# Wide matmuls beside the attention in the shape of the value matmuls, and another rule for the order of TensorE's work

## The chip, the cores and the metric

The kernel runs on one core of a Trainium2 chip. The metric is device time in microseconds for one execution, the median of several runs. Five engines run side by side, each its own instructions in order: TensorE (PE; its weight loads are shown apart as PEld), ScalarE (ACT), VectorE (DVE), GpSimd (POOL) and SyncE (SP), which here issues the DMAs. They wait for each other through semaphores.

## The reference

One pre-norm transformer layer on x of 2048 rows by 1024, in bf16. What is computed:

```
h  = x + attention(layernorm(x)) @ wo        # 32 heads of 32, softmax over all 2048 keys
h2 = h + gelu_tanh(layernorm(h) @ w1 + b1) @ w2 + b2     # hidden width 3584
```

The scores are `q.k * 32**-0.5`, without a mask; the layer norms have no weights.

## The kernel before

**A planner writes the order.** The kernel is not a loop over tiles that the engines follow. Python code records tasks one by one for each engine; a `Plan` holds for each engine the time until which it is planned (`plan.free`) and for each buffer its last writer and readers, and so says from when a task could start (`plan.ready`). Each task has a cost in ns written by hand. The costs decide only the order in which instructions stand; on the chip each engine runs its list in that order and waits on semaphores.

**Stages.** First come the layer norm of x, the transposes of its rows and the first projections (to about 58 us). Then comes the attention, in four chunks of 512 queries (`CH`), each with 16 pairs of heads. All other large products are laid beside it as filling: in the first chunk the remaining projections of keys, values and queries (`fill0`, line 838); in each later chunk the output projection, the layer norm and the feed-forward part of the chunk before (`ffn`, line 1144), for the first two also the queries of a later chunk (`late_queries`). What is left and the last chunk's output projection and feed-forward part follow behind the attention as the tail.

**A unit of scores** (`qk`, line 975) is up to three matmuls of 32 contraction rows and 128 keys by 512 queries, on different rows of the array, each into a PSUM bank of its own. A pair of heads has eleven units: ten of three banks and one of two. Banks 0 to 2 and 3 to 5 take turns. One exponential on ScalarE (line 994) reads a unit's banks and writes a slot of `PT`, of which there are six. So the scores of unit u+1 can start once the exponential of unit u-1 is done with its banks.

**A value group** (`pv`, line 1008) is four matmuls of 128x32 (128 contraction rows, 32 output columns) that stand beside each other in the array, at column positions 0, 32, 64 and 96, and write four quarters of bank 6: V of two heads, and ones for the two sums of the softmax. 16 such groups make a pair of heads; then VectorE takes the bank out (`finish_pair`).

**A wide matmul** is one of 128x128 by 512. `group` (line 516) records the eight of a projection or of a hidden block of the feed-forward part, two at a time; the 28 of an output block of the feed-forward part stand in `ffn` (line 1406); one of 128 columns is in `spread` (line 642), which with `sumsq` makes the norms that the bias of the exponential needs. Beside the attention all of these share one bank, 7: the next group waits until the bank has been taken out.

**Kinds.** `pe` (line 279) records a TensorE task with a kind: "R" for scores, "C" for value groups and `sumsq`, "F" for all else. Where the kind differs from the one before, the planner adds 105 ns.

**The loop** (from line 1444) chooses the next piece of TensorE's work. It works out `q_r`, `p_r` and `f_r`: when the next scores, value group and filling could start. Filling is given out in runs of at least `FMIN` (2) pieces unless the scores are more than `LATE` (700 ns) late; scores go when their banks are free; after scores, value groups go in runs if at least `CMIN` (4) are ready, else filling; and the earliest if none is ready. If the oldest value group not done is `NPT` (6) units back, value groups go first ("block"). `qk_prereq` (line 962) makes sure, by running filling until it is there, that the norms of a new group of heads are known, and issues the DMAs of the queries (`Qd`). From the second chunk on, `quota` holds filling back once the output projection is done.

Of the kernel before, what the change touches and what calls it, by code (L numbers as in the profile page):

```python
# [8 lines left out]
ACT = mybir.ActivationFunctionType  # L9
ALU = mybir.AluOpType  # L10
AX = mybir.AxisListType
E = mybir.EngineType

P = 128
INF = float("inf")
# [186 lines left out]
def build_kernel(nc, A_x, A_wqkv, A_wo, B_w1, B_b1, B_w2, B_b2, out):  # L202
    _, S, D = A_x.shape
    F = B_w1.shape[1]
    DH = 32
    NT = S // P
# [4 lines left out]
    FC = F // P  # L211
# [5 lines left out]
    GK = GC * math.sqrt(2.0 / math.pi)  # L217
    QF = 1.2
    EARLY = 8
    RES = (1, 2, 3)  # L220
    FMIN, LATE, CMIN = 2, 700.0, 4
    CH = [(0, 512), (512, 512), (1024, 512), (1536, 512)]

    x2 = A_x[0]
# [51 lines left out]

    work = [0.0]

    def pe(fn, reads=(), writes=(), inc=True, cost=0.0, kind="F"):
        if kind == "F":  # L280
            work[0] += cost
        if mode[0] != kind:
            cost += 105.0
            mode[0] = kind
        plan.task(E.PE, fn, reads=reads, writes=writes, inc=inc, cost=cost)

    def mm(n):
        return n / 2.4 + 2.5


    base = (nc.sbuf_base + 63) // 64 * 64
# [27 lines left out]
    biasm, _ = sb("biasm", [P, G, NCH], dt.float32)  # L319
    B_bias = [[Buf() for _ in range(NCH)] for _ in range(G)]  # L320
# [63 lines left out]
    B_ps = nbufs(8)  # L384
# [131 lines left out]
    def group(mms, evac, reads_of, n=512, chunk=2, chs=()):  # L516
        bank = fbanks.next()
        k = len(mms)
        for i, (lhsT, rhs) in enumerate(mms):
            if i % chunk == 0:  # L520
                rd = []
                for j in range(i, min(k, i + chunk)):
                    rd += reads_of(j)
                yield Need(rd, [B_ps[bank]] if i == 0 else [], [c_ for c_ in chs if c_ is not None] if i == 0 else ())
            pe(lambda p, i=i, lhsT=lhsT, rhs=rhs: p.matmul(ps[:, bank, 0:n], lhsT, rhs, start=(i == 0), stop=(i == k - 1)),  # L525
               reads=reads_of(i), writes=[B_ps[bank]] if i in (0, k - 1) else [], inc=(i == k - 1), cost=mm(n))
            if i == k - 1:
                evac(bank)

# [112 lines left out]
    def spread(n_ap, B_n, out_ap, B_out, cols):  # L642
        d_ = dgi[0] % 2
        dgi[0] += 1
        bank = fbanks.next()
        dve(lambda v: v.tensor_scalar(dg[:, d_, :], ident[:], n_ap, None, ALU.mult), reads=[B_ident, B_n], writes=[B_dg[d_]], cost=230)
        yield Need([B_dg[d_]], [B_ps[bank]])
        pe(lambda p: p.matmul(ps[:, bank, 0:P], ones_pp[:], dg[:, d_, :], start=True, stop=True),
           reads=[B_ones, B_dg[d_]], writes=[B_ps[bank]], cost=mm(P))
        dve(lambda v: v.tensor_reduce(out_ap, ps[:, bank, 0:P].rearrange("p (a b) -> p a b", a=cols), AX.X, ALU.max),  # L650
            reads=[B_ps[bank]], writes=[B_out], cost=290)

# [322 lines left out]
    def qk(u):  # L975
        ci, p_, un = units[u]
        w = CH[ci][1]
        g, tc = p_ // 2, CH[ci][0] // 512
        s0 = 3 * (u % 2)
        s = qdl[(ci, p_)]  # L980
        banks = sorted({b for _, _, b, _ in un})
        wr = [B_ps[s0 + b] for b in banks]
        n = len(un)
        for i, (kt, h, b, o) in enumerate(un):
            rg = h + 2 * (kt % 2)
            pe(lambda p, kt=kt, rg=rg, b=b, o=o: p.matmul(  # L986
                ps[:, s0 + b, o:o + w], K2[32 * rg:32 * rg + 32, p_, kt // 2, :], Qd[32 * rg:32 * rg + 32, s, 0:w],
                start=True, stop=True, tile_position=(32 * rg, 0), skip_group_check=True),
                reads=[B_Qd[s][0], B_Qd[s][1], B_K2h[p_][kt // 4][kt % 2]],
                writes=wr if i in (0, n - 1) else [], inc=(i == n - 1), cost=mm(w) if i % 3 == 0 else 4, kind="R")  # L990
        o_ = u % NPT
        nb = len(banks)
        wa = 512 if n != 2 or w == 512 else w
        act(lambda a: a.activation(PT[:, o_, 0:nb, 0:wa], ps[:, s0:s0 + nb, 0:wa], ACT.Exp, bias=biasm[:, g, tc:tc + 1], scale=SCALE),  # L994
            reads=wr + [B_bias[g][tc]], writes=[B_PT[o_]], cost=180 + 0.833 * nb * wa)
        for kt, h, b, o in un:
            kts.setdefault((ci, p_, kt), {})[h] = (u, b, o)
            if len(kts[(ci, p_, kt)]) == 2:
                d_ = kts.pop((ci, p_, kt))
                pending.append((ci, p_, kt, d_[0], d_[1]))  # L1000
# [143 lines left out]
    def ffn(ci, tail):  # L1144
# [163 lines left out]
        def hidden(fc, c0, c1):  # L1308
# [7 lines left out]
            def evac(bank):  # L1316
# [12 lines left out]
                else:  # L1329
                    st.append((E.DVE, lambda v: v.tensor_tensor(tm[gs][:, 0:n], xh[:, gs, 0:n], xh[:, gs, 0:n], ALU.mult), [Bx], [Bt], 80 + .65 * n))  # L1330
                st.append((E.DVE, lambda v: v.scalar_tensor_tensor(tm[gs][:, 0:n], tm[gs][:, 0:n], GB, xh[:, gs, 0:n], ALU.add, ALU.mult),  # L1331
                           [Bt, Bx], [Bt], 80 + 1.2 * n))
                st.append((E.Activation, lambda a: a.activation(tm[gs][:, 0:n], tm[gs][:, 0:n], ACT.Tanh, scale=GK), [Bt], [Bt], 180 + .75 * n))  # L1333
                st.append((E.DVE, lambda v: v.scalar_tensor_tensor(gT[:, fc, c0:c1], tm[gs][:, 0:n], 1.0, xh[:, gs, 0:n], ALU.add, ALU.mult),  # L1334
                           [Bt, Bx], B_out, 80 + 1.2 * n))
                g_ch[(fc, c0)] = chain(st)
# [57 lines left out]
        for hf in range(2):  # L1394
            turns = []
            for d4 in range(4):
                db = hf * 4 + d4
                s = w2s[db]
                bank = fbanks.next()
                for fc in range(FC):  # L1400
                    if fc == 6:
                        load_w2(db + len(B_w2_) - 1)
                    if fc % 2 == 0:
                        yield Need(B_gT[fc] + B_gT[fc + 1] + [B_w2_[s]], [B_ps[bank]] if fc == 0 else [],
                                   [g_ch[k_] for u_ in (fc, fc + 1) for k_ in ((u_, 0), (u_, 256)) if k_ in g_ch])
                    pe(lambda p, fc=fc, s=s, bank=bank: p.matmul(ps[:, bank, 0:w], w2[:, s, fc, :], gT[:, fc, 0:w],  # L1406
                                                                 start=(fc == 0), stop=(fc == FC - 1)),
                       reads=B_gT[fc] + [B_w2_[s]], writes=[B_ps[bank]] if fc in (0, FC - 1) else [], inc=(fc == FC - 1), cost=mm(w))
                dve(lambda v, bank=bank, db=db: v.tensor_scalar(oT[:, db, 0:w], ps[:, bank, 0:w], b2f[:, db:db + 1], None, ALU.add),  # L1409
                    reads=[B_ps[bank], Bf_b2f], writes=[B_oT[db]], cost=690)  # L1410

                def turn(db=db, hf=hf, d4=d4):
                    dma_t(ost[:, hf * 4:hf * 4 + 4, d4 * P:(d4 + 1) * P], oT[:, db, :], 131072, [B_oT[db]], [B_od[db]])
                turns.append(chain([("call", turn, [B_oT[db]], [B_od[db]], 0)]))
# [21 lines left out]

    fbanks.items = [7]
    fbanks.i = 0
    state["gens"].append(fill0())
    state["left"] = (8 * len(v_left) + 7 * 32 + 3 * 64 + 12 * 8) * mm(512)  # L1440
    u = 0
    ph = 0
    seg, nf = None, 0
    while u < NU or pending:
        t = plan.free[E.PE]
        service(t)
# [27 lines left out]
                break  # L1474
        quota = state["left0"] * QF * (u - state["u0"] + 1) / state["nu"] + 2000.0
        f_r = fill_ready() if (ph == 0 or ("wo", ph - 1) not in marks or state["left0"] - state["left"] < quota) else INF
        def pvs(n):
            for _ in range(max(1, n)):
                pv()

        if block:
            pvs(npv)
            seg = "C"
            continue
        late = t - q_r
        if seg == "F" and nf < FMIN and f_r <= t + 60 and late < LATE:
            nf += 1
            do_fill()
            continue
        if q_r <= t + 60:  # L1490
            qk(u)
            u += 1
            seg, nf = None, 0
            continue
        if seg is None:
            ends = npv and pending[npv - 1][2] == NT - 1
            if npv >= CMIN or ends or (npv >= 2 and f_r > t + 100):
                pvs(npv)
                seg = "C"
                continue  # L1500
            if f_r <= t + 100:
                do_fill()
                seg, nf = "F", 1
                continue
        elif seg == "F":
            if f_r <= t + 60:
                do_fill()
                nf += 1
                continue
        elif f_r <= t + 60 and q_r > t + 350:  # L1510
            do_fill()
            seg, nf = "F", 1
            continue
        best = min(q_r, p_r if p_r + 330 < q_r or q_r == INF else INF, f_r)
        if best == INF:
            if pending:
                pv()
                seg = "C"
            elif not do_fill():
                raise RuntimeError("stuck")  # L1520
        elif best == q_r:
            qk(u)
            u += 1
            seg, nf = None, 0
        elif best == f_r:
            do_fill()
            seg, nf = "F", 1
        else:
            pvs(npv)
            seg = "C"  # L1530

    rings = [([7, 6], 0), ([0, 1, 2, 3, 4, 5], 0)]
    both = [state, dict(state, gens=deque([ffn(len(CH) - 1, True)]), need=None, gen=None)]
# [113 lines left out]
```

## Time and profile before

| | |
|---|---|
| median of 3 runs | 1227.95 us (1225.98 to 1229.10) |
| the profiled execution | 1226.59 us, its span 1224.8 us |
| mean granted TensorE clock | 0.993 |
| TensorE, ScalarE, VectorE, GpSimd busy | 1185.8, 1116.5, 646.5, 26.8 us |
| exponentials (line 994) | 704, 995.9 us busy, first start 58.2, last end 1105.8 us |
| value matmuls (line 1023) | 2048 with V and 2048 with ones |
| score matmuls (line 986) | 2048 |
| TensorE instructions | 9297 matmuls, 9297 weight loads |

Busy time is the union of the instructions' times. On TensorE and ScalarE an instruction begins before the one ahead of it has ended, so the length of one is more than its price in a row of equal ones: that is read from the distance of their starts. "Idle before" is the time in which the engine stood still ahead of an instruction, and the name behind the arrow is the instruction that ended it.

### The profile page before, as it was taken

The numbers are of one execution on the slowest core, as the hardware profiler recorded it, in microseconds if no ns is written. First come the engines' busy times: TensorE is split into PE (matmuls) and PEld (weight loads), VectorE is DVE, ScalarE is ACT, GpSimd is POOL, SyncE is SP. The second block draws the span as 40 slices with busy tenths as digits, with TensorE's granted clock in tenths as the row PEclk, the third lists the DMA queues.
The fourth block names the chain that finished last, engine by engine and source line by source line (L and its number), as shares of the span: only waits on it lengthen the run. The fifth ranks groups of instructions, "written<-read, shape, count | busy, mean of one in ns | idle before, by whom it ended". The sixth has DMA issues, their size and how long they took to land.

```text
span 1224.8 us, 22862 instructions
## 1 busy us (share of the span) xinstructions
PE 1185.8 (97%) x9297; PEld 406.3 (33%) x9297; DVE 646.5 (53%) x1228; ACT 1116.5 (91%) x927; POOL 26.8 (2%) x132
## 2 busy tenths in 40 slices
PE   4999999999999999999999999999999999999999
PEld 2433323233233333333233333333223333325544
DVE  7734444444565888222366885223567852327851
ACT  5799999999999999999999999999999999994830
POOL 1100000000010000000010000000100000000000
PEclk9999999999999999999999999999989999998999
DMA  7253322223341234343622351542322613424921
GB/s 227 49 135 71 73 53 57 57 54 102 70 87 57 79 93 101 78 117 78 170 60 78 90 138 33 108 112 59 89 78 73 158 42 74 101 60 147 288 73 52
DMA packets 294840, 113.96 MB, mean 93 GB/s; under 512 B 206928, under 2 KB 292048, under 8 KB 294736
## 3 DMA queue, kind: packets, MB, share of 16 engines
q1 hardware_dynamic: 294736, 112.51, 35.8%
q8 instruction: 73, 1.20, 0.4%
q14 instruction: 31, 0.25, 0.1%
HBM read 85.21 MB, written 4.19 MB: 73 GB/s over the span
## 4 chain that ended last, share of the span: by engine, by line
PE 81%; DVE 8%; ACT 5%; issue 3%; SPq 1%; DMA 1%; POOL 0%; DVEq 0%; ACTq 0%
PE ps L525 30%; PE ps L1023 17%; PE ps L986 15%; PE ps L1406 13%; ACT PT L994 5%; PE ps L1378 4%; SPq L256 1%; DVE lnst L462 1%; DVE xh L1324 1%; DVE QT L1053 1%; DVE Rg L1043 1%; PE ps L1216 1%; DVE tm L1331 0%; DVE Rg L1049 0%; PE ps L505 0%
## 5 line engine op out<-in xcount | busy, mean ns | idle before, releaser
L994 ACT ACTIVATE PT<-ps,biasm 128x1536 bf16<-128x1536 f32 (+1 forms) x704 | 995.9, 1538 | 13.4 <-PE ps L986 12.1
L1023 PE MATMUL ps<-PT,V 128*32 128x512 bf16 x2048 | 285.5, 385 | 0.3 <-ACT PT L994 0.2
L1023 PE MATMUL ps<-PT,ones 128*32 128x512 bf16 x2048 | 285.8, 386 | 0.0
L986 PE MATMUL ps<-Qd,K 32*128 32x512 bf16 x2048 | 275.3, 386 | 7.7 <-ACT PT L994 6.1
L525 PE MATMUL ps<-hnT,w 128*128 128x512 bf16 x672 | 173.1, 382 | 3.4 <-DVE xh L1324 2.9
L1406 PE MATMUL ps<-gT,w 128*128 128x512 bf16 x672 | 173.2, 382 | 0.3 <-DVE xh L1324 0.3
L986 PEld LDWEIGHTS ps<-Qd,K 32*128 32x128 bf16 x2048 | 68.1, 91 | 297.0 <-issue 156.4
L1023 PEld LDWEIGHTS ps<-PT,V 128*32 128x32 bf16 x2048 | 77.7, 95 | 138.4 <-issue 87.5
L1036 DVE COPY Sg<-ps 128x512 f32<-128x512 f32 x64 | 44.3, 692 | 146.9 <-PE ps L1023 146.9
L525 PE MATMUL ps<-xnTe,wk 128*128 128x512 bf16 x384 | 98.6, 387 | 3.2 <-ACT xnTe L567 1.3
L1324 DVE TENSOR_SCALAR xh<-ps,b1f 128x512 bf16<-128x512 f32 x84 | 63.0, 750 | 50.1 <-PE ps L525 49.6
L525 PEld LDWEIGHTS ps<-hnT,w 128*128 128x128 bf16 x672 | 52.9, 97 | 91.0 <-issue 35.6
L1406 PEld LDWEIGHTS ps<-gT,w 128*128 128x128 bf16 x672 | 52.4, 97 | 81.3 <-issue 34.7
L1023 PEld LDWEIGHTS ps<-PT,ones 128*32 128x32 bf16 x2048 | 78.0, 95 | 0.4
L1409 DVE TENSOR_SCALAR oT<-ps,b2f 128x512 bf16<-128x512 f32 x24 | 18.0, 751 | 113.3 <-PE ps L1406 113.2
L525 PE MATMUL ps<-xnTl,wk 128*128 128x512 bf16 x256 | 65.3, 381 | 0.4
L1331 DVE SCALAR_TENSOR_TENSOR tm<-tm,xh 128x512 bf16<-128x512 bf16 x84 | 58.0, 691 | 2.4
L1334 DVE SCALAR_TENSOR_TENSOR gT<-tm,xh 128x512 bf16<-128x512 bf16 x84 | 57.1, 684 | 2.7 <-ACT tm L1333 2.4
L1333 ACT ACTIVATE tm<-tm 128x512 bf16<-128x512 bf16 x84 | 54.3, 650 | 3.8 <-DVE tm L1331 3.5
L525 PE MATMUL ps<-hnT,w_t 128*128 128x512 bf16 (+1 forms) x288 | 48.8, 332 | 0.0
L525 PEld LDWEIGHTS ps<-xnTe,wk 128*128 128x128 bf16 x384 | 31.9, 99 | 50.8 <-issue 20.8
L1378 PE MATMUL ps<-w_t,gT 128*128 128x512 bf16 (+1 forms) x252 | 48.6, 355 | 0.0
(121 smaller groups left out, 798.1 us busy)
## 6 DMA issues: line engine op xcount, KB each, us to landing
w<-in_B_w_dram SPq DMA_DIRECT2D x42, 512.0 KB, 3.8
w<-in_B_w_dram SPq DMA_DIRECT2D x24, 896.0 KB, 5.7
wk<-in_A_wqkv_dram SPq DMA_DIRECT2D x32, 256.0 KB, 3.8
Qd<-QT SPq DMA_DIRECT2D x128, 64.0 KB, 2.6
w_t<-in_B_w_dram SPq DMA_DIRECT2D x14, 512.0 KB, 6.5
w_t<-in_B_w_dram SPq DMA_DIRECT2D x8, 896.0 KB, 7.2
xr<-in_A_x_dram SPq DMA_DIRECT2D x16, 256.0 KB, 5.2
K<-kst SPq DMA_DIRECT2D x128, 32.0 KB, 1.9
```

Of the source, the lines that this page charges most:

```text
L525: pe(lambda p, i=i, lhsT=lhsT, rhs=rhs: p.matmul(ps[:, bank, 0:n], lhsT, rhs, start=(i == 0), stop=(i == k - 1)), reads=reads_of(i), write ...
L986: pe(lambda p, kt=kt, rg=rg, b=b, o=o: p.matmul(ps[:, s0 + b, o:o + w], K2[32 * rg:32 * rg + 32, p_, kt // 2, :], Qd[32 * rg:32 * rg + 32, ...
L994: act(lambda a: a.activation(PT[:, o_, 0:nb, 0:wa], ps[:, s0:s0 + nb, 0:wa], ACT.Exp, bias=biasm[:, g, tc:tc + 1], scale=SCALE), reads=wr ...
L1023: pe(lambda p, c0=c0, lhsT=lhsT, uu=uu, b=b, o=o: p.matmul(ps[c0:c0 + 32, OD, 0:w], lhsT, PT[:, uu % NPT, b, o:o + w], start=start, stop=stop,
L1036: dve(lambda v: v.tensor_copy(Sg[:, pr, 0:w], ps[:, OD, 0:w]), reads=[B_ps[OD]], writes=[B_Sg[pr]], cost=690)
L1324: dve(lambda v: v.tensor_scalar(xh[:, gs, 0:n], ps[:, bank, 0:n], b1f[:, fc:fc + 1], 0.5, ALU.add, ALU.mult), reads=[B_ps[bank], Bf_b1f], ...
L1331: st.append((E.DVE, lambda v: v.scalar_tensor_tensor(tm[gs][:, 0:n], tm[gs][:, 0:n], GB, xh[:, gs, 0:n], ALU.add, ALU.mult), [Bt, Bx], [Bt ...
L1333: st.append((E.Activation, lambda a: a.activation(tm[gs][:, 0:n], tm[gs][:, 0:n], ACT.Tanh, scale=GK), [Bt], [Bt], 180 + .75 * n))
L1334: st.append((E.DVE, lambda v: v.scalar_tensor_tensor(gT[:, fc, c0:c1], tm[gs][:, 0:n], 1.0, xh[:, gs, 0:n], ALU.add, ALU.mult), [Bt, Bx], ...
L1378: pe(lambda p, fc=fc, bank=bank, c0=c0, c1=c1, hf=hf, rows=rows: p.matmul(ps[:, bank, 0:c1 - c0], gT[:, fc, rows], w2h[hf][0][:, fc, c0:c1 ...
L1406: pe(lambda p, fc=fc, s=s, bank=bank: p.matmul(ps[:, bank, 0:w], w2[:, s, fc, :], gT[:, fc, 0:w], start=(fc == 0), stop=(fc == FC - 1)), r ...
L1409: dve(lambda v, bank=bank, db=db: v.tensor_scalar(oT[:, db, 0:w], ps[:, bank, 0:w], b2f[:, db:db + 1], None, ALU.add), reads=[B_ps[bank], ...
```

## The change

The change has three parts.

1. Beside the attention (`narrow[0]` is true from before the loop until after it) every wide matmul that opens a bank there is recorded by a new function `wide` as four of 128x32, at the four column positions, with the same moving operand and a quarter of the weights each. They write the four quarters of the bank and have the kind "C", that of the value groups. A bank that was opened in one form is finished in it.
2. The loop loses its runs. Scores go as soon as their banks are free by the plan; then value groups if the oldest not done is five units back (`LAG`) or the next one ends a pair of heads; then filling; and the earliest if none is ready. Value groups go one at a time.
3. Costs of the planner: 97 in place of 105 ns for a change of kind, 145 + 0.8333 per element in place of 180 + 0.833 for an exponential, 95 + 0.83 in place of 180 + 0.75 for a tanh. The three further matmuls of a wide one cost the planner nothing.

```diff
@@ -218,7 +218,7 @@
     RES = (1, 2, 3)
-    FMIN, LATE, CMIN = 2, 700.0, 4
+    LAG = 5
@@ -276,16 +276,31 @@
-    def pe(fn, reads=(), writes=(), inc=True, cost=0.0, kind="F"):
-        if kind == "F":
+    def pe(fn, reads=(), writes=(), inc=True, cost=0.0, kind="F", fill=False):
+        if kind == "F" or fill:
             work[0] += cost
         if mode[0] != kind:
-            cost += 105.0
+            cost += 97.0
             mode[0] = kind
...
+    narrow = [False]
+    opened = {}
+
+    def wide(bank, c0, n, lhsT, rhs, start, stop, reads, writes, inc):
+
+        if start:
+            opened[bank] = narrow[0]
+        if not opened[bank]:
+            pe(lambda p: p.matmul(ps[:, bank, c0:c0 + n], lhsT, rhs, start=start, stop=stop), reads=reads, writes=writes, inc=inc, cost=mm(n))
+            return
+        for c in range(4):
+            pe(lambda p, c=c: p.matmul(ps[32 * c:32 * c + 32, bank, c0:c0 + n], lhsT[:, 32 * c:32 * c + 32], rhs, start=start, stop=stop,
+                                       tile_position=(0, 32 * c), skip_group_check=True),
+               reads=reads, writes=writes if c in (0, 3) else [], inc=inc and c == 3, cost=mm(n) if c == 0 else 0, kind="C", fill=True)
@@ -522,8 +537,7 @@
-            pe(lambda p, i=i, lhsT=lhsT, rhs=rhs: p.matmul(ps[:, bank, 0:n], lhsT, rhs, start=(i == 0), stop=(i == k - 1)),
-               reads=reads_of(i), writes=[B_ps[bank]] if i in (0, k - 1) else [], inc=(i == k - 1), cost=mm(n))
+            wide(bank, 0, n, lhsT, rhs, i == 0, i == k - 1, reads_of(i), [B_ps[bank]] if i in (0, k - 1) else [], i == k - 1)
@@ -645,8 +659,7 @@
-        pe(lambda p: p.matmul(ps[:, bank, 0:P], ones_pp[:], dg[:, d_, :], start=True, stop=True),
-           reads=[B_ones, B_dg[d_]], writes=[B_ps[bank]], cost=mm(P))
+        wide(bank, 0, P, ones_pp[:], dg[:, d_, :], True, True, [B_ones, B_dg[d_]], [B_ps[bank]], True)
@@ -992,7 +1005,7 @@
-            reads=wr + [B_bias[g][tc]], writes=[B_PT[o_]], cost=180 + 0.833 * nb * wa)
+            reads=wr + [B_bias[g][tc]], writes=[B_PT[o_]], cost=145 + 0.8333 * nb * wa)
@@ -1330,7 +1343,7 @@
-                st.append((E.Activation, lambda a: a.activation(tm[gs][:, 0:n], tm[gs][:, 0:n], ACT.Tanh, scale=GK), [Bt], [Bt], 180 + .75 * n))
+                st.append((E.Activation, lambda a: a.activation(tm[gs][:, 0:n], tm[gs][:, 0:n], ACT.Tanh, scale=GK), [Bt], [Bt], 95 + .83 * n))
@@ -1403,9 +1416,8 @@
-                    pe(lambda p, fc=fc, s=s, bank=bank: p.matmul(ps[:, bank, 0:w], w2[:, s, fc, :], gT[:, fc, 0:w],
-                                                                 start=(fc == 0), stop=(fc == FC - 1)),
-                       reads=B_gT[fc] + [B_w2_[s]], writes=[B_ps[bank]] if fc in (0, FC - 1) else [], inc=(fc == FC - 1), cost=mm(w))
+                    wide(bank, 0, w, w2[:, s, fc, :], gT[:, fc, 0:w], fc == 0, fc == FC - 1,
+                         B_gT[fc] + [B_w2_[s]], [B_ps[bank]] if fc in (0, FC - 1) else [], fc == FC - 1)
@@ -1436,11 +1448,11 @@
+    narrow[0] = True
...
@@ -1474,60 +1486,35 @@
...
         if block:
-            pvs(npv)
-            seg = "C"
+            pv()
             continue
-        late = t - q_r
-        if seg == "F" and nf < FMIN and f_r <= t + 60 and late < LATE:
-            nf += 1
-            do_fill()
-            continue
         if q_r <= t + 60:
             qk(u)
             u += 1
-            seg, nf = None, 0
             continue
-        if seg is None:
-            ends = npv and pending[npv - 1][2] == NT - 1
-            if npv >= CMIN or ends or (npv >= 2 and f_r > t + 100):
-                pvs(npv)
-                seg = "C"
-                continue
...
+        oldest = min(pending[0][3][0], pending[0][4][0]) if pending else u
+        first_c = npv and (u - oldest >= LAG or pending[npv - 1][2] == NT - 1)
+        if first_c and p_r <= t + 60:
+            pv()
+            continue
+        if f_r <= t + 60:
             do_fill()
-            seg, nf = "F", 1
             continue
-        best = min(q_r, p_r if p_r + 330 < q_r or q_r == INF else INF, f_r)
+        best = min(q_r, p_r, f_r)
...
-        else:
-            pvs(npv)
-            seg = "C"
+    narrow[0] = False
```

More of the change, by code (lines that the diff above doesn't have):

```diff
@@ L1476, in build_kernel @@
         f_r = fill_ready() if (ph == 0 or ("wo", ph - 1) not in marks or state["left0"] - state["left"] < quota) else INF
-        def pvs(n):
-            for _ in range(max(1, n)):
-                pv()
         if block:
-            pvs(npv)
-            seg = "C"
-            continue
-        late = t - q_r
-        if seg == "F" and nf < FMIN and f_r <= t + 60 and late < LATE:
-            nf += 1
-            do_fill()
+            pv()
             continue
@@ L1492, in build_kernel @@
             u += 1
-            seg, nf = None, 0
             continue
-        if seg is None:
-            ends = npv and pending[npv - 1][2] == NT - 1
-            if npv >= CMIN or ends or (npv >= 2 and f_r > t + 100):
-                pvs(npv)
-                seg = "C"
-                continue
-            if f_r <= t + 100:
-                do_fill()
-                seg, nf = "F", 1
[L1504 to L1510, printed above, removed]
+        oldest = min(pending[0][3][0], pending[0][4][0]) if pending else u
[4 more added lines that the diff above has]
+        if f_r <= t + 60:
             do_fill()
-            seg, nf = "F", 1
             continue
-        best = min(q_r, p_r if p_r + 330 < q_r or q_r == INF else INF, f_r)
+        best = min(q_r, p_r, f_r)
         if best == INF:
@@ L1523, in build_kernel @@
             u += 1
-            seg, nf = None, 0
-        elif best == f_r:
+        elif best == p_r:
+            pv()
+        else:
             do_fill()
-            seg, nf = "F", 1
-        else:
-            pvs(npv)
-            seg = "C"
+    narrow[0] = False
     rings = [([7, 6], 0), ([0, 1, 2, 3, 4, 5], 0)]
```

## The prediction

> **What bounds the kernel now.** I read the page first (engine shares, clock slices, the chain), then ScalarE's timeline and waits, then TensorE's timeline, then a table of short windows around the two dips of the clock.
>
> ```profile
> span 1224.8 us, 22862 instructions
> ...
> PE 1185.8 (97%) x9297; PEld 406.3 (33%) x9297; DVE 646.5 (53%) x1228; ACT 1116.5 (91%) x927; POOL 26.8 (2%) x132
> ...
> PEclk9999999999999999999999999999989999998999
> ...
> q8 instruction: 73, 1.20, 0.4%
> ...
> PE 81%; DVE 8%; ACT 5%; issue 3%; SPq 1%; DMA 1%; POOL 0%; DVEq 0%; ACTq 0%
> ...
> L994 ACT ACTIVATE PT<-ps,biasm 128x1536 bf16<-128x1536 f32 (+1 forms) x704 | 995.9, 1538 | 13.4 <-PE ps L986 12.1
> ```
>
> The chain puts 81% on TensorE, but ScalarE is just as full beside the attention. Its timeline (start, length, count):
>
> ```profile
> 432.20 2.95 ACT L994 ACTIVATE PT<-ps,biasm 128x1536 bf16<-128x1536 f32 x2
> 435.05 0.63 ACT L1333 ACTIVATE tm<-tm 128x512 bf16<-128x512 bf16 x1
> 435.57 2.97 ACT L994 ACTIVATE PT<-ps,biasm 128x1536 bf16<-128x1536 f32 x2
> 438.41 0.64 ACT L1333 ACTIVATE tm<-tm 128x512 bf16<-128x512 bf16 x1
> ...
> 499.08 61.51 ACT L994 ACTIVATE PT<-ps,biasm 128x1536 bf16<-128x1536 f32 x44 [0.19 <-PE ps L986]
> ```
>
> Two exponentials go from 435.57 to 438.41, so one starts 1.423 us after the other; the lengths overlap. A tanh takes 0.52 (435.05 to 435.57), an exponential over two banks 0.996. The page's 704 are 640 of three banks and 64 of two, and 84 tanh lie among them: 640 x 1.423 + 64 x 0.996 + 84 x 0.520 = 1018.1 us. The first exponential starts at 58.2, the last ends at 1105.8: 1047.6. So 29.3 us are lost there. Taking each start against the shortest distance, 18.8 of them stand before exponentials released by scores (the waits show 12.1 of that as idle), 6.1 before tanh released by VectorE, 4.3 are a few ns per instruction.
>
> TensorE's timeline:
>
> ```profile
> 400.25 0.39 PE L986 MATMUL ps<-Qd,K 32*128 32x512 bf16 x3
> 400.57 0.60 PE L525 MATMUL ps<-hnT,w 128*128 128x512 bf16 x2
> 401.11 0.39 PE L1023 MATMUL ps<-PT,V 128*32 128x512 bf16 x2
> 401.12 0.39 PE L1023 MATMUL ps<-PT,ones 128*32 128x512 bf16 x2
> 401.34 0.38 PE L1023 MATMUL ps<-PT,V 128*32 128x512 bf16 x2
> 401.34 0.38 PE L1023 MATMUL ps<-PT,ones 128*32 128x512 bf16 x2
> 401.55 0.38 PE L1023 MATMUL ps<-PT,V 128*32 128x512 bf16 x2
> 401.56 0.38 PE L1023 MATMUL ps<-PT,ones 128*32 128x512 bf16 x2
> 401.87 0.39 PE L986 MATMUL ps<-Qd,K 32*128 32x512 bf16 x3
> ```
>
> Groups of one kind follow each other after 0.216 us, the first pair of a run after 0.226; this holds for one 128x128 matmul and for four 128x32 alike. Wherever the kind changes the distance is 0.31 to 0.32 (scores 400.25, wide 400.57), so a change costs 0.09 to 0.11, 0.105 where scores are on one side. In the built order of before I count, between the first score and the last value matmul, 1580 changes. With those distances TensorE has 1007 us of work there, 1016 with the 10 ns: as much as ScalarE's 1018. Neither has slack, and each stall of one costs the other.
>
> Windows (TensorE, its loads, VectorE, ScalarE, GpSimd, granted clock, DMA):
>
> ```profile
> 884.00:888.00 4.00, 2.75 (x35) 0.70 (x31) 1.03 (x3) 4.00 (x4) 2.00 (x11) 1.00 0.00 0
> 888.10:894.90 6.80, 6.19 (x36) 1.22 (x33) 1.78 (x4) 6.80 (x5) 0.24 (x2) 0.50 0.42 96
> 1099.70:1109.90 10.20, 9.52 (x53) 2.18 (x46) 3.17 (x6) 6.14 (x5) 0.00 (x0) 0.50 0.24 78
> ```
>
> Where wide work had run out (TensorE busy 2.75 of 4.00 us) the clock was halved soon after.
>
> **Kind changes.** The built order of the changed kernel has 1399 changes in place of 1580, all between scores and the rest: 181 x 0.105 = 19 us less on TensorE. Wide matmuls in that stretch fall from 2172 to 2144. Pricing the new order with the same distances gives 983 us, 990 with the 10 ns per run, against ScalarE's unchanged 1018. By query chunk (new TensorE / ScalarE): 238/243, 249/258, 251/258, 246/258. Pair of heads by pair, the sum of the larger of the two is 1027 before and 1020 now.
>
> **Four for one.** 2144 wide matmuls become 8576 narrow ones, with as many weight loads. At 0.216 a group this costs nothing; the row for it is the value matmuls, same shape, same array tiles, no slower in their fifth group than in their second. Bounds: -0.003 (by the rows' spread) and +0.010 us a group, the distance between the first and the third start of a group (401.11, 401.12), were it not hidden: 21 us. I take 0, the back-to-back row being the nearest. The Trainium skill (TensorE: Matmul & The Clock Gate, Measured speedup vs the span model) gives four packed matmuls a span of one plus some 4 ns for each further one, 12 ns; on every group that would be an estimated 26 us. This trace shows the offset inside a group, but not in the distance of groups.
>
> **Scores as soon as a bank is free.** This moves no work; it moves when ScalarE is served. Losses of over 0.4 us before an exponential are ten, together 10.7 us: one is the clock (0.64 at 895), the others lie where the order has two score units back to back, both banks drained, or where a norm or a DMA forces them. The order of before has ten such double units after the first, the new one three (units 132, 176, 554). Unit 176 cost 1.9 before, the mean is 1.07; I take 1.7 each, 5.1, and 0.6 for the clock, which units 576 to 584, with one or two value groups each and no wide work, should halve again. The other 8.1 us are small; they go with the saturated pairs, whose excess over ScalarE falls from 9 to 2, so I keep 2.7. Of 18.8, 8.4 stay: 10.4 saved. Bounds: 18.8 if all goes, 0 if the stalls only move. Scores now wait at the head of TensorE's queue, with values and wide work behind them; a late tanh (6.1, kept) stops TensorE too, which its 27 us of slack cover. Values may lag five units of six PT slots; one slot is left, about 1.4 us, against 0.43 for two groups, so I cost it at nothing.
>
> **The tail.** One whole output block of the third chunk's feed-forward, 28 wide matmuls, is left and goes after the attention as 128x128: 28 x 0.216 = 6.0 us. TensorE has no gap there before (busy to 1221.9), so all of it counts. After the last scores stand 15 groups (2 value, 8 wide, 5 value), 3.4 us, against 2.4 of exponentials: TensorE ends 1.0 after ScalarE, 0.6 before (1106.44): +0.4. Wide work now runs to the end, so the dip at 1099.7 should not come; of it 4.1 us at half speed lay behind the last exponential, with 0.2 on the last value group: -2.2. Sum +4.2.
>
> **Other edits.** The planner's new costs for exponential and tanh change only the order, counted above. DMAs, their queues and VectorE's instructions keep their number; SP's queue is moved past nothing. Instructions fetched rise from 1.20 MB by 15783/9297 to 2.0 MB: a packet every 8 us in place of 16; nothing in the trace waits for one.
>
> **Sum.** 1226.6 (the profiled execution, span 1224.8 and 1.8 around it) - 10.4 + 4.2 = 1220.4. It lies 1.4 below the median of the three runs, 1227.95 (1225.98 to 1229.10). I predict 1221. Under 0.3%, 3.7 us, I call it no change.
>
> **Rivals.**
>
> The stalls only move (chance 0.17). Norms and late Qd transfers force scores in both orders, as at unit 176. For it: the largest three losses (2.3, 2.2, 1.9) are of that sort. Against: three drained places for ten. Then 1226.6 + 4.2 = 1231 at worst, 1227 with half the gain.
>
> The offset adds (0.09). If the 10 ns inside a group came on top of each narrow group, TensorE has 990 + 21 = 1011 us, the balance of before, and the gain goes: about 1230. Against: the back-to-back rows. The Trainium skill's rule above (same page and section) leads here too; by its 12 ns the estimate is 1235.
>
> TensorE can't be fed (0.16, slower). A narrow group takes eight instructions in 0.216 us; before, a unit of scores, values and wide work had about 24 in 1.42 us, now 43. If issue or fetch is slower in the long run than in the short bursts of value matmuls, the groups stretch. With 0.030 us more, 64 us, TensorE has 1054 and bounds: with the 18 us of other losses kept, 1072 in place of 1047.6, so 1226.6 + 24 + 4 = 1255. It decides from about 0.013 a group, where TensorE's work is level with ScalarE's 1018 again and only the tail's +4.2 is left. Against: no growth within a run of five; nothing in the trace tells of longer ones, which now go to nine.
>
> Half clock for longer (0.06). If units 576 to 584 bring two or three dips of 6.8 to 10.2 us, with wide work queued behind, each costs up to 5 us: 1224 to 1230.
>
> **Chances.** My own case has 0.52, by itself 1214 to 1225. 0.46 of it and small parts of the first and last rivals (0.06) give faster 0.52; its other 0.06, most of those two rivals (0.15) and two thirds of the offset (0.06) give no change 0.27; the feeding rival, the last third of the offset and the worst of the moved stalls give slower 0.21. Range 1212 to 1235: under it lies the case that all 18.8 go, above it most of the feeding rival.
>
> **What would show it.** In the changed profile: narrow wide groups 0.216 us apart, in long runs too; exponentials 1.423 apart with the idle time before them down from 13.4 to about 6; first to last exponential about 1037; a half clock near units 576 to 584 and none at the end; 28 of the block's matmuls after the last exponential. Groups over 0.23 apart, or ScalarE waiting for value matmuls, would make me wrong.

## The result: slower by 0.7%

The median went from 1228.53 to 1236.69 us (1236.32 to 1237.70), a ratio of 1.0071 with a 95% interval of [1.0053, 1.0088]. The forecast was 1221, in a range of 1212 to 1235: wrong in sign. The page of the changed kernel, in the lines that answer to those shown before:

```profile
span 1234.6 us, 35830 instructions
...
PE 1189.8 (96%) x15783; PEld 428.2 (35%) x15783; DVE 647.9 (52%) x1228; ACT 1117.2 (90%) x927; POOL 26.6 (2%) x132
...
PEclk9999999999999999999999999999989999999999
...
q8 instruction: 124, 2.03, 0.7%
...
PE 81%; DVE 12%; ACT 3%; issue 2%; DMA 1%; POOL 0%; SPq 0%; DVEq 0%; ACTq 0%
...
L1007 ACT ACTIVATE PT<-ps,biasm 128x1536 bf16<-128x1536 f32 (+1 forms) x704 | 996.3, 1545 | 15.0 <-PE ps L999 10.7
```

The chain now has 12% on VectorE in place of 8%, and the idle time before exponentials is 15.0 us in place of 13.4. From the first to the last exponential it takes 1050.9 us (58.3 to 1109.2) in place of 1047.6; from there to the end 125.4 in place of 119.0. So of 9.8 us between the two profiled executions (1236.4 and 1226.6), 3.3 lie beside the attention and 6.4 behind it.

The narrow groups are not what costs. A run of eight wide matmuls in TensorE's timeline, between value groups:

```profile
1107.37 0.38 PE L1036 MATMUL ps<-PT,V 128*32 128x512 bf16 x2
1107.38 0.38 PE L1036 MATMUL ps<-PT,ones 128*32 128x512 bf16 x2
1107.59 1.90 PE L301 MATMUL ps<-gT,w 128*32 128x512 bf16 x32
1109.31 0.38 PE L1036 MATMUL ps<-PT,V 128*32 128x512 bf16 x2
```

From 1107.59 to 1109.31 there are eight groups, 0.215 us each: no offset and no growth. What TensorE now does more often stands in a stretch of the first feed-forward block (start, length, engine, line; idle time before in brackets):

```profile
440.37 0.60 PE L301 MATMUL ps<-hnT,w 128*32 128x512 bf16 x6
...
441.03 0.75 DVE L1337 TENSOR_SCALAR xh<-ps,b1f 128x512 bf16<-128x512 f32 x1 [1.11 <-PE ps L301]
...
441.44 0.39 PE L1036 MATMUL ps<-PT,V 128*32 128x512 bf16 x2
...
441.83 0.12 PEld L301 LDWEIGHTS ps<-hnT,w 128*32 128x32 bf16 x8 [0.29 <-DVE xh L1337]
441.84 0.40 PE L301 MATMUL ps<-hnT,w 128*32 128x512 bf16 x4
```

The last wide group in bank 7 starts at about 440.59, VectorE begins to take the bank out 0.43 later and is done at 441.78, and the next filling starts at 441.84, right behind it. Behind the value group of 441.44 it could have started at 441.66: 0.18 us of TensorE's time lost. Call it an evacuation when VectorE takes bank 7 out. Over the attention I took each start of a group on TensorE against the shortest distance for its kinds and summed what an evacuation of bank 7 released: 7.4 us before, 24.0 after. (The sum depends on where the line is drawn: all first groups that start within 0.16 us of an evacuation's end give 10 and 33.) Of the next fillings 18 of 207 started within 75 ns of the evacuation's end before, 83 of 205 after. And the waits reach ScalarE: before, ten exponentials lost over 0.4 us, 10.7 us together, and ahead of the scores of one of them TensorE had waited for bank 7; in the changed kernel seventeen did, 14.4 us together, and ten of them had such a wait ahead.

For a hidden block of the feed-forward part the planner reckons from the last matmul's start to the next filling 216 (matmul) + 90 (hop) + 714 (evacuation) + 90 (hop) = 1110 ns. The trace has 433 from the last matmul's start to the evacuation where VectorE was idle (417 with whole wide matmuls), some 742 for the evacuation (751 for a hidden block, 691 for most others, which the planner reckons with 690) and at least 53 to the next matmul: 1228. The bank is ready some 0.12 us later than planned, and all of that lies ahead of the evacuation, 433 against 306: from its start on, 751 + 53 = 804 ns are just what was planned. The new loop gives out filling as soon as the plan says it is ready (up to 60 ns ahead of that, `f_r <= t + 60`); the old one had mostly put something else there.

### The profile page after: what moved, and what is told of

It reads as the page before. It is cut to its first block, busy times and chain, and to the rows that moved or that the text cites. A ratio compares the mean times of both kernels' runs of the same rounds, so it can differ in the third digit from the quotient of the medians.

```text
span 1234.6 us, 35830 instructions
## 1 busy us (share of the span) xinstructions
PE 1189.8 (96%) x15783; PEld 428.2 (35%) x15783; DVE 647.9 (52%) x1228; ACT 1117.2 (90%) x927; POOL 26.6 (2%) x132
## 3 DMA queue, kind: packets, MB, share of 16 engines
q8 instruction: 124, 2.03, 0.7%
## 4 chain that ended last, share of the span: by engine, by line
PE 81%; DVE 12%; ACT 3%; issue 2%; DMA 1%; POOL 0%; SPq 0%; DVEq 0%; ACTq 0%
PE ps L301 36%; PE ps L1036 19%; PE ps L999 15%; PE ps L298 6%; PE ps L1391 4%; ACT PT L1007 2%; DVE Rg L1056 2%; DVE xh L1337 1%; DVE Sg L1049 1%; DVE lnst L477 1%; DVE QT L1066 1%; DVE tm L1344 1%; DVE Rg L1062 1%; DVE rcp L1059 1%; DVE gT L1347 0%
## 5 line engine op out<-in xcount | busy, mean ns | idle before, releaser
L1007 ACT ACTIVATE PT<-ps,biasm 128x1536 bf16<-128x1536 f32 (+1 forms) x704 | 996.3, 1545 | 15.0 <-PE ps L999 10.7
L1036 PE MATMUL ps<-PT,V 128*32 128x512 bf16 x2048 | 330.0, 386 | 0.8 <-DVE Sg L1049 0.4
L1036 PE MATMUL ps<-PT,ones 128*32 128x512 bf16 x2048 | 330.2, 386 | 0.0
L301 PE MATMUL ps<-hnT,w 128*32 128x512 bf16 x2688 | 176.8, 382 | 5.0 <-DVE xh L1337 3.0
L301 PE MATMUL ps<-gT,w 128*32 128x512 bf16 x2576 | 173.2, 380 | 0.9 <-DVE oT L1421 0.6
L1036 PEld LDWEIGHTS ps<-PT,V 128*32 128x32 bf16 x2048 | 80.6, 95 | 142.5 <-issue 113.0
L301 PEld LDWEIGHTS ps<-hnT,w 128*32 128x32 bf16 x2688 | 63.1, 96 | 81.9 <-issue 25.0
L301 PEld LDWEIGHTS ps<-gT,w 128*32 128x32 bf16 x2576 | 62.8, 96 | 66.6 <-issue 9.5
L301 PE MATMUL ps<-xnTe,wk 128*32 128x512 bf16 x1184 | 79.3, 381 | 1.5 <-DVE kst L637 0.5
L301 PE MATMUL ps<-xnTl,wk 128*32 128x512 bf16 x864 | 58.5, 381 | 0.5 <-DVE kmax L663 0.2
L600 DVE CAST kst<-ps 128x512 bf16<-128x512 f32 x28 | 19.3, 691 | 57.6 <-PE ps L301 57.5
```

Of the source, the lines that this page charges most:

```text
L301: pe(lambda p, c=c: p.matmul(ps[32 * c:32 * c + 32, bank, c0:c0 + n], lhsT[:, 32 * c:32 * c + 32], rhs, start=start, stop=stop, tile_posit ...
L1036: pe(lambda p, c0=c0, lhsT=lhsT, uu=uu, b=b, o=o: p.matmul(ps[c0:c0 + 32, OD, 0:w], lhsT, PT[:, uu % NPT, b, o:o + w], start=start, stop=stop,
```

## Experiments

The theory (bank): the narrow groups are free, and the saving is lost in these waits. Rivals: the narrow shape hurts in itself (shape), or the new planner costs spoil the order (costs). In the table "attention" is from the first to the last exponential's end, "behind" from there to the span's end, "bank" the waits for evacuations of bank 7, worked out as above; all three are of the profiled execution. Ratios are to the kernel before as it ran beside each kernel; its medians there were 1226.2 to 1228.5. In the traces of "before, held 120 ns", "changed, held, wide whole" and "before, new costs" some 150 wide matmuls are not recorded: the 6.1 of the first is rough, and "bank" stays open for the other two, as for the last two kernels.

| kernel | median us | ratio to before | attention | bank | behind |
|---|---|---|---|---|---|
| before | 1228.5 | | 1047.6 | 7.4 | 119.0 |
| changed | 1236.7 | 1.0071 [1.0053, 1.0088] | 1050.9 | 24.0 | 125.4 |
| old order, narrow | 1222.5 | 0.9954 [0.9935, 0.9972] | 1044.6 | 11.4 | 118.7 |
| changed, held 120 ns | 1221.9 | 0.9961 [0.9946, 0.9976] | 1038.3 | 8.1 | 123.6 |
| changed, held 300 ns | 1222.2 | 0.9962 [0.9949, 0.9975] | 1038.6 | 7.5 | 122.7 |
| changed, old costs | 1244.0 | 1.0138 [1.0123, 1.0153] | 1065.5 | 31.4 | 118.2 |
| before, held 120 ns | 1225.7 | 0.9981 [0.9970, 0.9992] | 1046.7 | 6.1 | 119.2 |
| changed, held, wide whole | 1250.3 | 1.0182 [1.0166, 1.0198] | 1066.6 | | 123.9 |
| old loop, narrow, new costs, held | 1221.2 | 0.9950 [0.9934, 0.9966] | 1042.8 | 9.2 | 118.2 |
| before, new costs | 1231.3 | 1.0034 [1.0025, 1.0043] | 1041.6 | | 129.2 |
| old loop as above, queries earlier | 1220.6 | 0.9951 [0.9935, 0.9968] | 1042.8 | | 119.2 |
| changed, held, queries earlier | 1223.3 | 0.9974 [0.9965, 0.9983] | 1040.1 | | 123.4 |

**The narrow shape alone, in the old order.** `wide` of the change put into the kernel before; for the planner all four keep the old kind, the first with the cost of a whole one, so that nothing moves.

```diff
+        for c in range(4):
+            pe(lambda p, c=c: p.matmul(ps[32 * c:32 * c + 32, bank, c0:c0 + n], lhsT[:, 32 * c:32 * c + 32], rhs, ...),
+               ..., cost=mm(n) if c == 0 else 0, kind="F")
```

> The order of before, instruction for instruction, with each wide matmul beside the attention as four of 128x32 in its place (the planner still counts it as a wide one, so no task moves). On the array the changes between wide and value work vanish: 1385 in place of 1580, 195 x about 0.1 = 19 us less for TensorE (991 against 1008 from the built orders). Bank theory (the narrow groups are free; the changed kernel lost its saving in waiting for the evacuation of bank 7, because the new loop gives out filling the moment the planner says and the planner says so about 0.12 us too early): the old order keeps other work between two fillings, so most of the saving comes through, 1217 to 1224 against 1228.5 before. Shape theory (narrow wide groups themselves hurt: they end later, load worse or crowd the others): no faster than before, 1228 to 1236. Cost theory (the planner's new costs spoilt the order): says the same as the bank theory here.

1222.5, faster by 0.46%: the shape theory falls. Yet 195 changes fewer, 19 us of TensorE's work, brought 3.0 us beside the attention in the profiled execution (1223.7, near the slow end of four) and some 5 to 6 in the medians. ScalarE still loses 26.3 us there (29.3 before), 17.7 of them before exponentials that scores ended: in the same order, the norms and DMAs that force scores stay where they were, and the waits for bank 7 rose by 4.0.

**Filling held in the planner.** In the changed kernel, a piece of filling that opens a bank counts as ready 120 or 300 ns later.

```diff
-        return plan.ready(E.PE, nd.reads, nd.writes)
+        return plan.ready(E.PE, nd.reads, nd.writes) + (120.0 if nd.writes and narrow[0] else 0.0)
```

> The changed kernel, but the planner holds a piece of filling that opens a bank for 120 ns longer; that is the distance by which the trace's chain (last matmul of a group to the first of the next in bank 7: 433 + 742 + 53 = 1228 ns) exceeds the planner's 1110. Bank theory: TensorE's waits for evacuations in the attention fall from 24 us to 8 to 14, next fillings within 0.15 us of an evacuation's end from 151 of 205 to under 90, time 1226 to 1233 (1236.7 unheld). Shape and cost theories: no change, 1235 to 1238, as 22 wide matmuls are still left for the tail in place of 28.

> As with 120, but held for 300 ns. Bank theory: waits for evacuations under 6 us, time 1223 to 1231, no worse than with 120. Shape and cost theories: 1235 to 1238, or slower, since filling is given out later for nothing (16 wide matmuls left for the tail).

1221.9 and 1222.2. Both beat the expectation of the bank theory, and the two rivals fall. The waits drop from 24.0 to 8.1 and 7.5; fillings within 75 ns of the evacuation from 83 to 25 and 16. (Two numbers missed: with 120 ns I had expected under 90 fillings within 0.15 us, and 99 came; with 300 ns under 6 us of waits.) The attention takes 1038.3, 12.6 less than unheld. Unheld, about 4 us of that were lost before exponentials to scores, 3.3 to a late norm and 4.6 before tanh. Held, nine exponentials lost over 0.4 us, and ahead of none of them had TensorE waited for bank 7. The hold also moves other pieces of the order (22 wide matmuls are left for the tail, not 28), so that the whole 12.6 us come from these waits isn't shown; that the hold pays and that the waits fall with it is. The same place in the block with 120 ns:

```profile
436.18 0.61 PE L301 MATMUL ps<-hnT,w 128*32 128x512 bf16 x8
...
436.84 0.75 DVE L1337 TENSOR_SCALAR xh<-ps,b1f 128x512 bf16<-128x512 f32 x1 [0.69 <-PE ps L301]
...
437.61 0.39 PE L1036 MATMUL ps<-PT,V 128*32 128x512 bf16 x2
...
437.71 0.23 PEld L301 LDWEIGHTS ps<-hnT,w 128*32 128x32 bf16 x8
...
437.83 0.39 PE L301 MATMUL ps<-hnT,w 128*32 128x512 bf16 x4
```

Value groups fill the evacuation until 437.59, and the next filling starts 0.22 behind the last of them, without a wait. The exponentials' row, held:

```profile
L1007 ACT ACTIVATE PT<-ps,biasm 128x1536 bf16<-128x1536 f32 (+1 forms) x704 | 997.8, 1593 | 10.6 <-PE ps L999 9.4
```

**The planner's old costs in the changed kernel.**

```diff
-            cost += 97.0
+            cost += 105.0
...
-            ..., cost=145 + 0.8333 * nb * wa)
+            ..., cost=180 + 0.833 * nb * wa)
...
-                ..., 95 + .83 * n))
+                ..., 180 + .75 * n))
```

> The changed kernel with the three planner costs of before (105, 180 + 0.833, 180 + 0.75). By the built order nothing of the feed-forward block is left for the tail (641 matmuls there, as before, in place of 669). Bank theory: waits for evacuations stay above 18 us and the first to last exponential at 1048 us or more; only the tail's 6 us are won, less what the attention now takes for 28 more wide matmuls: 1230 to 1238. Cost theory: the loss goes, 1222 to 1229.

1244.0, slower than both theories allowed. The costs theory falls outright: the new costs were worth 7 us. The bank theory had its 31.4 us of waits, but not how far the attention would grow, to 1065.5: that is 14.6 us more for 7.4 us more of waits. ScalarE's losses beside the attention, tanh included, rise from 32.6 to 47.1, those before exponentials that scores ended from 16.3 to 27.4. The exponentials' row has more waits for scores in it:

```profile
L1007 ACT ACTIVATE PT<-ps,biasm 128x1536 bf16<-128x1536 f32 (+1 forms) x704 | 1001.9, 1518 | 17.8 <-PE ps L999 15.9
```

What fits, though only argued: an exponential that the planner takes for 1.46 us (180 + 0.833 x 1536) while the chip takes 1.423 lets it lay more work between two scores than there is room for.

**The hold on the kernel before.** The same line in the old loop, nothing else.

> The kernel before (wide matmuls whole, old loop, old costs) with filling that opens bank 7 held 120 ns longer by the planner, and nothing else. Bank theory: the old loop waits little for evacuations (7 us in the attention, 36 of 207 next fillings within 0.15 us of an evacuation's end), so there is little to win: 1223 to 1230 against 1227.4. If the hold is simply good for any order, whatever the loop, it gains here as much as on the changed kernel (about 1%): 1213 to 1218.

1225.7, faster by 0.19%, in the expected range. The hold repairs the new loop (1.2%); in the old one it is worth little.

**Whole wide matmuls in the new order.** The changed kernel, held, with one matmul in place of the four; the order is the same.

```diff
-        for c in range(4):
-            pe(lambda p, c=c: p.matmul(ps[32 * c:32 * c + 32, ...], lhsT[:, 32 * c:32 * c + 32], rhs, ...), ..., kind="C", fill=True)
+        pe(lambda p: p.matmul(ps[:, bank, c0:c0 + n], lhsT, rhs, start=start, stop=stop),
+           reads=reads, writes=writes, inc=inc, cost=mm(n), kind="C", fill=True)
```

> The changed kernel with the 120 ns hold, but each wide matmul whole (128x128) on the array again, in exactly the same order (the planner still counts it as of the value groups' kind). By the built order 1857 changes of kind in place of 1395: 462 x 0.1 = 44 us more for TensorE (1032 against 989), above ScalarE's 1018. If four for one is free and saves the changes: TensorE bounds, first to last exponential 1060 to 1085 in place of 1038, time 1243 to 1268. If narrow groups carried a cost of their own of 0.01 us or more (21 us): half of that or less, 1222 to 1240.

1250.3, attention 1066.6: 28 us more for 44 us of changes, as expected if four for one is free. In this order the narrow shape is worth 2.3%.

```profile
L1005 ACT ACTIVATE PT<-ps,biasm 128x1536 bf16<-128x1536 f32 (+1 forms) x704 | 1000.0, 1521 | 27.2 <-PE ps L997 23.6
```

**The old loop with everything else.** The first experiment's kernel, with the four told to the planner as kind "C", the new costs and the 120 ns hold.

> The loop of before with four narrow matmuls for a wide one, told to the planner as of the value groups' kind, with the new costs and the 120 ns hold. By the built order 1391 changes and nothing of the feed-forward block left for the tail. If the rule of the new loop (scores at once, values singly) brings nothing beyond fewer changes, this should reach 1038 to 1042 from first to last exponential with a tail of 118 to 119: 1215 to 1220. If the new loop's rule is what keeps scores on time, it stays near the old order with narrow matmuls: 1220 to 1225.

1221.2: in the second expectation, near its lower end. The attention takes 1042.8, 4.5 more than in the new loop held, but nothing is left for the tail, 118.2 behind it in place of 123.6. The two come out within each other's interval: what the new loop wins beside the attention it hands back as wide matmuls that are left over. That it serves ScalarE better by its rule doesn't follow. One wait for queries, before the exponential at 607.7, costs the old loop 5.3 us, more than the whole difference, and the new loop held has none there:

```profile
607.26 0.75 PE L999 MATMUL ps<-Qd,K 32*128 32x512 bf16 x6 [2.35 <-DMA Qd<-QT]
```

**The new costs in the kernel before.**

```diff
-            cost += 105.0
+            cost += 97.0
...
-            ..., cost=180 + 0.833 * nb * wa)
+            ..., cost=145 + 0.8333 * nb * wa)
```

(and the tanh's, as in the change)

> The kernel before with the planner's three costs of the change (97, 145 + 0.8333, 95 + 0.83) and nothing else; 1557 changes in place of 1580. The changed kernel lost 7 us when it got the old costs, because a planner that takes an exponential for 1.46 us where the chip takes 1.423 lays too much of TensorE's work between two scores. If that holds for the old loop too, losses before exponentials fall: 1219 to 1225 against 1227.4. If the old loop is guarded by its own runs, no change: 1225 to 1230.

1231.3, a miss. The attention did shrink, by 6.0 to 1041.6, but 10 us more lie behind it. TensorE's timeline from the last scores on shows where, and two lines of SP's say why:

```profile
1098.74 0.39 PE L986 MATMUL ps<-Qd,K 32*128 32x512 bf16 x2
1099.06 5.35 PE L1406 MATMUL ps<-gT,w 128*128 128x512 bf16 x24
...
1111.26 0.39 PE L1224 MATMUL ps<-wo(1, 0)_99,QT 128*128 128x512 bf16 x1 [1.23 <-DVE QT L1053]
...
1127.31 7.08 PE L525 MATMUL ps<-hnT,w_t 128*128 128x256 bf16 x48 [3.85 <-DMA w_t<-in_B_w_dram]
```

```profile
1108.99 14.31 SPq L256 DMA_DIRECT2D out_dram<-ost  x4
1123.34 5.80 SPq L256 DMA_DIRECT2D w_t<-in_B_w_dram  x5
```

24 wide matmuls stand ahead of the last value groups, and the values' chain on VectorE, which the tail needs, comes that much later: with the waits that follow, 4.8 of the 10.3 us. The rest has another cause. SP issued the tail's weights only at 1123.34, behind four stores of results; in the kernel before, where the stores went out at 1098.4, it did so at 1108.8. TensorE waited 3.85 us for them, and the next 48 matmuls, partly at half clock, took 1.7 us longer than before. So the attention's 6.0 us came back in part as work that TensorE had left over, and in part by an order on SP that was not among the expectations. No other kernel here has such a wait for the tail's weights.

**Queries loaded earlier.** In the old loop with everything else and in the changed kernel held for 120 ns, the DMA of the queries of a chunk's second pair is also recorded at the last pair of the chunk before.

```diff
             qd_load(*((ci, p_ + 1) if p_ + 1 < NP else (ci + 1, 0)))
+            if p_ + 1 == NP and ci + 1 < len(CH):
+                qd_load(ci + 1, 1)
```

> The old loop with narrow matmuls, new costs and the hold, as before, and beside that the queries of a chunk's second pair are loaded already when the last pair of the chunk before starts, so that their DMA stands ahead of the seven weight loads which SP issues at the chunk's start. In the run without this the exponentials lost 7.0 us between 600 and 650, one wait of 5.2 us before scores that waited for Qd. If that DMA is the cause and nothing else is late next: 4 to 6 us less, 1214 to 1218. If other work takes the wait's place (TensorE has no slack to use): within 2 us of 1221.2.

> The changed kernel with the 120 ns hold and the same earlier load of queries. There the exponentials lost only 0.6 us between 600 and 650, so there is nothing to win there: 1219 to 1224 against 1221.9.

1220.6 and 1223.3: no gain in the old loop, the number of the second expectation, and none in the new, as expected. The loss between 600 and 650 stayed, 7.6 us. SP's timeline there, in the old loop:

```profile
590.68 12.43 SPq L256 DMA_DIRECT2D wq<-in_A_wqkv_dram  x7
603.16 2.74 SPq L256 DMA_DIRECT2D Qd<-QT  x4
```

The edit moved the wrong pair. The exponential that waits is the first of the chunk's third pair (unit 374; the chunk begins with unit 352), while the second pair's queries had been issued by 562.2 already without the edit, well ahead of the weight loads. The queries of the third and fourth pair still stand behind the seven loads. So this run tests neither expectation: the trace names the DMA as the cause of the wait, and what it would bring to issue it earlier wasn't tried.

## Why the prediction was wrong

**Kind changes, and four for one at nothing: right.** 1399 changes and 0.215 us a group; whole matmuls in the same order cost 28 us. The offset rival and the feeding rival fall, the latter with eight groups in a row at full pace. The Trainium skill's 4 ns for each further tile (TensorE: Matmul & The Clock Gate, Measured speedup vs the span model) is seen inside a group, whose four matmuls mostly start 0, 3 to 4, 7 and 10 ns after the first, and not between groups.

**Scores as soon as a bank is free, 10.4 saved: this step failed.** It said the rule "moves no work" and kept 8.4 of the 18.8 us that scores cost the exponentials. 16.3 stayed, and 3.3 more stood behind the late norm at unit 176, priced at 1.7 (1.9 before, among the 18.8), so nothing of the 18.8 was saved. With 8.1 before tanh, where 6.1 were kept, the attention took 1050.9; the step's own sum says 1037.2. I priced TensorE's new order by the distances of its starts, 990 us, and compared that with ScalarE's 1018, as if TensorE never stood still. Its waits for bank 7, 7.4 us before, had no term; they became 24.0, most of the 27 us of slack that I had counted on. With the hold, which lowers them to 8.1, the attention takes 1038.3, close to the step's sum: the term that I had left out is worth up to 12.6 us. That the held kernel's 1221.9 meets the forecast is in part luck, as its losses are not the ones I had kept: some 12 us before exponentials, where the forecast has 8.4, and 3.5 before tanh, where it has 6.1. The trace of before had the numbers for the missing term: the chain over bank 7, beside the planner's costs.

**The tail, +4.2: mis-sized; it was 6.4.** 28 wide matmuls were left, and no half clock came at the end, as said. The end lay 1.3 us behind the last exponential to the first output projection in place of 0.6 (+0.7, forecast +0.4); the slow stretch gave 1.7 and not 2.2; and the rest, 1.3, are two waits that I had not looked for, for VectorE's last values and for a DMA (0.38 and 0.62 us idle; 0.55 and 0.79 by the starts):

```profile
1115.59 0.39 PE L1237 MATMUL ps<-wo(1, 0)_99,QT 128*128 128x512 bf16 x1 [0.38 <-DVE QT L1066]
...
1117.89 0.39 PE L298 MATMUL ps<-hch,ident 128*128 128x512 bf16 x1 [0.62 <-DMA hch<-in_A_x_dram]
...
1128.51 5.34 PE L298 MATMUL ps<-gT,w 128*128 128x512 bf16 x24
```

**Other edits, nothing: wrong in size.** The planner's costs are worth 7 us in the new loop and cost 4 in the old, where the late weights in the tail alone make 5.5. (Instructions fetched came to 2.03 MB, as forecast; in 124 packets that is one every 10 us, and the forecast's 8 was a slip.)

**The clock: right.** One half-clock stretch, where wide work had run out near unit 576:

```profile
912.00:915.00 3.00, 1.66 (x18) 0.42 (x18) 2.87 (x6) 3.00 (x3) 0.00 (x0) 1.00 0.01 3
915.00:925.20 10.20, 9.35 (x69) 1.94 (x69) 2.15 (x6) 9.92 (x8) 2.34 (x12) 0.50 0.29 66
```

Of the rivals, "the offset adds" came nearest in time with the higher of its figures, 1235, but only by luck: the groups follow each other at 0.215 us. "The stalls only move", at its worst 1231, was nearest in kind and named the wrong stalls: for the most part not the forced scores but a bank in places where little had been waited for.

## What to carry to other kernels

Where a change lets work start "as soon as it is ready", look up what ready means to whoever decides it, and hold it against the whole chain in the trace, from the start of the last writer to the first start after: here 0.12 us too early, some 150 times, took back most of a saving of 19 us. An order's cost on an engine is its instructions and its waits for what it shares, here one bank. Where two engines are equally full, look for time won on one in the work left over on the other: in the new loop held, 4.5 us less beside the attention than in the old loop stand against 5.4 more behind it. And look through the whole trace before a loss gets its name: twice it was a DMA that stood in SP's queue behind others.

## What the runs showed of the hardware

In the kernel before, a change between 128x128 and 128x32 tiles costs TensorE about as much (0.09 to 0.11 us above the 0.216 of a run) as one to the 32-row tiles of the scores. Four 128x32 matmuls of one moving operand run at the pace of one 128x128, 0.215 us in the changed kernel. There the clock was halved from 915.0 on, after 3.00 us in which TensorE was busy for 1.66. And four matmuls in place of one make their reader start 16 ns later (433 against 417 ns from the last one's start).
